# Two interleaved attention and gated-MLP layers on one core: four maxima products together in the lean steps, with three smaller moves in the order

## The chip, the cores and the metric

The kernel runs on one core of a Trainium2 chip. The metric is device time in microseconds (us) for one execution; the kernel before took 2261.78 us (median of 3 runs, 2261.09 to 2262.83).

## What is computed

Two pairs of blocks on x of 2048 x 448, every block with a layer norm before it and a residual after it:

```python
x = x + attention(layernorm(x))   # 16 heads of 28; one key and one value head for all
x = x + (sigmoid(n @ w_gate) * (n @ w_up)) @ w_down   # n = layernorm(x), 1792 wide
# attention: softmax over 2048 keys of (q . k) * 28 ** -0.5, times v, times wo
# and both blocks once more
```

The weights of both layers are the same.

## The kernel before

**Units and steps.** A layer's attention is worked in 16 units of 128 queries (`u`), each in 16 steps of 128 keys (`kt`): 256 steps a layer. A step has four score products, one for a group of four heads (`scores`: tile `s`, line 566; 96 rows deep, because queries and keys are split into high and low halves), four exponentials on ScalarE (`P`, line 570) and four products with the values (`pv`, line 584), of the step before.

**Maxima.** The softmax needs each query's largest score before its unit starts. So beside a unit's steps the next unit's approximate scores are made, 32 rows deep: one group of four heads and 512 keys a step, four products `mx` (line 509; the four heads lie on four row strips of TensorE, `tile_position`), each reduced by VectorE over 512 columns (line 512). `mx_gen` yields after two of the four, so that `next(mx)` is half a group and `group(mx)` a whole one. After 16 groups `maxima` takes the largest (lines 543, 544) and leaves `fin` in `late`; `finish` runs it: a transposition on TensorE (`mt`, line 549), a copy on VectorE (`mr`, line 551) and a DMA on SyncE's queue into row 92 of the next unit's queries `QS` (line 552), which that unit's first score product reads.

**The order.** All orders are written out by hand, and each engine and each DMA queue works in that order. Two strings stand for a pass of two steps: S is a score product, F a slice of other TensorE work (`fill`: query projections, the gated MLP's products), M a group of maxima, m half of one, P the value products, T `finish`, X the end of a step. `FULL` is used where there is much fill work, `LEAN` where there is little: in layer 0 for steps 0 to 49 and in layer 1 for steps 0 to 45, 48 passes of 256 in all. In unit 0 two steps have one more group (`MORE`).

**PSUM.** Score, maxima, fill and transposition tiles share seven PSUM buffers of one tag ("f"); a product waits until the buffer's last reader has finished. An eighth holds `pv`.

**Behind a unit.** Its sums go by stages, one a step (`tick`): `f0` and `fx` move the sums out and back by DMA to spread them, `fy` takes reciprocals (VectorE), `fz` and `fw` move them out and back broadcast (`lb`), `fa` multiplies `pvs` by them on GpSimd (line 675), `fb` splits the product (ScalarE, then VectorE), `fc` starts the product with `wo`. In layer 0's lean steps GpSimd also splits the gate and up weights (lines 154 to 156, 279).

**Queries.** `qproj` projects 512 queries of four heads; the high part is written by ScalarE (line 430) and the low part either by VectorE out of PSUM (line 440), or, where `by_pool` is set, by a second ScalarE write to SBUF (line 433) and GpSimd (line 438). In layer 1 two of its four blocks are projected in the lean steps.

## Time and profile before

| | |
|---|---|
| median of 3 runs | 2261.78 us |
| the profiled execution, its own time | 2257.6 us |
| its span on the core (first to last instruction) | 2255.8 us |
| TensorE busy | 2202.9 us, 98% |
| VectorE busy | 1673.9 us, 74% |
| ScalarE busy | 1397.3 us, 62% |
| GpSimd busy | 1045.8 us, 46% |

Busy time is the time in which an instruction of the engine is under way. TensorE's matmuls overlap, and their ends are modelled, so that a wait can hide in a busy row. In the rows PE is TensorE, PEld its weight loads, DVE is VectorE, ACT ScalarE, POOL GpSimd and SP SyncE; a q behind the name is the engine's DMA queue.

### The profile page before, as it was taken

To read this page: it belongs to the slowest core of one execution; us is meant where nothing else is said; L and a number is where in the kernel's file an instruction comes from. 1 tells how busy PE (TensorE), PEld (TensorE's weight loads), DVE (VectorE), ACT (ScalarE), POOL (GpSimd) and SP (SyncE) were. 2 spreads that over 40 slices of the span, in tenths; PEclk is the share of its full clock that TensorE was granted. 3 is DMA by queue.
4 is the path that set the end of the run, shared out by engine and by line. 5 is a ranking of instruction groups with operands and counts; after the bars stand their busy time and mean duration, and the time that the engine had idled before them with its cause. 6 is when DMAs were issued, how large, how long until landed. Compare 5 with 4: busy or idle time off the path is not lost. (4 is left out here: it accounts for less than half of the span.)

```text
span 2255.8 us, 43048 instructions
## 1 busy us (share of the span) xinstructions
PE 2202.9 (98%) x16336; PEld 1049.5 (47%) x16336; DVE 1673.9 (74%) x2921; ACT 1397.3 (62%) x2567; POOL 1045.8 (46%) x1363
## 2 busy tenths in 40 slices
PE   8999999999999999999999999999999999999999
PEld 6322244544545444454573224545454544445457
DVE  7898887878778887774458887878787877878322
ACT  4677766666666666666425676666666666666641
POOL 4378451555445554546402014545545455454540
PEclk9999999999999999999999999999999999999999
DMA  6734542323313232332341113223232313232233
GB/s 154 212 105 133 184 158 61 93 77 103 112 52 106 67 90 80 98 96 79 102 145 57 31 47 103 85 85 101 60 94 63 102 59 102 80 95 89 78 99 123
DMA packets 224400, 217.53 MB, mean 96 GB/s; under 512 B 154048, under 2 KB 185536, under 8 KB 224192
## 3 DMA queue, kind: packets, MB, share of 16 engines
q1 hardware_dynamic: 217200, 198.89, 30.0%
q0 software_dynamic: 3680, 12.09, 1.4%
q10 hardware_dynamic: 3312, 3.79, 0.5%
q8 instruction: 128, 2.10, 0.4%
q14 instruction: 80, 0.66, 0.1%
HBM read 175.37 MB, written 23.59 MB: 88 GB/s over the span
## 5 line engine op out<-in xcount | busy, mean ns | idle before, releaser
L570 ACT ACTIVATE P<-s 128x512 f32<-128x512 f32 x2048 | 1141.3, 599 | 565.0 <-PE s L566 544.7
L512 DVE TENSOR_REDUCE mp<-mx 128x1 f32<-128x512 f32 x2048 | 1266.7, 681 | 300.6 <-PE mx L509 295.4
L566 PE MATMUL s<-QS,KK 96*128 96x512 f16 x2048 | 740.3, 381 | 21.8 <-DVE mp L512 9.2
L369 PEld LDWEIGHTS <-wgu 128*128 128x128 f16 x4928 | 459.5, 97 | 254.1 <-issue 91.6
L604 POOL TENSOR_TENSOR PH<-P,PH 128x512 f16<-128x512 f32 x384 | 458.7, 1195 | 30.8
L603 POOL CAST PH<-P 128x512 f16<-128x512 f32 x384 | 248.5, 647 | 471.5 <-ACT P L570 471.5
L584 PE MATMUL pv<-P,VV 128*32 128x512 f32 x3328 | 418.5, 599 | 0.0
L369 PE MATMUL gp<-XT,wgu 128*128 128x256 f16 x2464 | 386.1, 272 | 0.8 <-DVE mp L512 0.7
L369 PE MATMUL up<-XT,wgu 128*128 128x256 f16 x2464 | 385.3, 272 | 1.1 <-ACT P L570 0.4
L789 PE MATMUL dn<-WD,h 128*128 128x448 f16 x1344 | 330.4, 353 | 0.0
L509 PE MATMUL mx<-KK,QH 32*128 32x512 f16 x2048 | 257.2, 384 | 5.1 <-ACT P L570 3.1
L566 PEld LDWEIGHTS <-KK 96*128 96x128 f16 x2048 | 188.4, 97 | 136.0 <-issue 62.3
L509 PEld LDWEIGHTS <-QH 32*128 32x128 f16 x2048 | 62.2, 91 | 344.8 <-issue 343.3
L789 PEld LDWEIGHTS <-h 128*128 128x128 f16 x1344 | 124.7, 98 | 138.6 <-issue 23.7
L584 PEld LDWEIGHTS pv<-P,VV 128*32 128x32 f32 x3328 | 86.4, 109 | 167.5 <-issue 146.3
L764 DVE SCALAR_TENSOR_TENSOR h<-th,h 128x512 f16<-128x512 f32 x112 | 99.5, 888 | 48.4 <-ACT h L763 48.4
L763 ACT ACTIVATE h<-th 128x512 f16<-128x512 f32 x112 | 70.3, 628 | 88.0 <-DVE th L760 86.9
L760 DVE SCALAR_TENSOR_TENSOR th<-th,up 128x512 f32<-128x512 f32 x112 | 76.0, 679 | 57.2 <-PE up L369 51.7
L675 POOL TENSOR_TENSOR lb<-pvs,lb 128x512 f32<-128x512 f32 x32 | 40.7, 1270 | 138.3 <-DMA lb<-sums 119.7
L752 ACT ACTIVATE th<-gp,gsc 128x512 f32<-128x512 f32 x112 | 76.8, 686 | 42.3 <-PE gp L369 41.8
L369 PE MATMUL qp<-XT,WQ 128*128 128x512 f16 x352 | 98.4, 386 | 0.7 <-DVE ktl L412 0.7
L329 POOL TENSOR_SCALAR rs<-mv 128x1 f32<-128x1 f32 x48 | 11.0, 229 | 178.6 <-DVE mv L324 178.6
(164 smaller groups left out, 1102.9 us busy)
## 6 DMA issues: line engine op xcount, KB each, us to landing
wgu<-wgu_d SPq DMA_DIRECT2D x224, 512.0 KB
QS<-qd SPq DMA_DIRECT2D x384, 32.0 KB
lb<-sums SPq DMA_DIRECT2D x120, 64.0 KB
wgu_d<-sgu POOLq DMA_DIRECT2D x14, 512.0 KB, 3.8
qd<-qst POOLq DMA_DIRECT2D x16, 256.0 KB, 2.7
xr<-in_A_x_dram SPq DMA_DIRECT2D x16, 224.0 KB
QH<-qd SPq DMA_DIRECT2D x28, 128.0 KB
x2d<-x SPq DMA_DIRECT2D x16, 224.0 KB
```

Of the source, the lines that this page charges most:

```text
L369: nc.tensor.matmul(ps, a, b, start=n == 0, stop=n == 10)
L509: nc.tensor.matmul(ps[h][:, :nk], qh[32 * h:32 * h + 32, g], KK[l][32 * h:32 * h + 32, 1, ks], start=True, stop=True, tile_position=(32 * ...
L512: nc.vector.tensor_reduce(mp[:, g, h, kb:kb + 1], ps[h][:, :nk], axis=AX.X, op=OP.max)
L566: nc.tensor.matmul(s, KK[l][0:96, 0, kt * 128:(kt + 1) * 128], QS[l, u][:, g].rearrange("p h n -> p (h n)"), start=True, stop=True)
L570: nc.scalar.activation(p, s, AF.Exp, scale=ESC)
L584: nc.tensor.matmul(v[32 * g:32 * g + 32], VV[l][:, kt], P[g], start=kt == 0, stop=kt == KT - 1, tile_position=(0, 32 * g))
L603: {"A": nc.scalar.copy, "V": nc.vector.tensor_copy, "P": nc.gpsimd.tensor_copy}[e](h[:, 0], p)
L604: nc.gpsimd.tensor_tensor(h[:, 1], p, h[:, 0], op=OP.subtract)
L752: defer(lambda: nc.scalar.activation(th, gp.rearrange("p j n -> p (j n)"), AF.Tanh, scale=gsc))
L760: nc.vector.scalar_tensor_tensor(t, th, 1.0, up.rearrange("p j n -> p (j n)"), op0=OP.add, op1=OP.mult)
L764: defer(lambda: nc.vector.scalar_tensor_tensor(h[:, 1], t, 2.0 ** -17, h[:, 0], op0=OP.mult, op1=OP.subtract), 1)
L789: nc.tensor.matmul(p, hs[f // 2][:, a, o:o + 128], WD[:, f, c], start=n == 0, stop=n == 3 * FC - 1)
```

## The change

Four edits. `LEAN` has a whole group M at the end of a step, where it had two halves m, one between the score products and one at the end. `finish` leaves `fin` alone until two steps have passed since the group that ended the maxima, except in the last pass of a unit. `fa` comes one step later for units 0 to 2 of each layer (`LU`). And `by_pool` holds for all projections by `qproj`, which moves 12 low parts from VectorE to ScalarE and GpSimd.

```diff
-        by_pool = l == 0 or b == 1
+        by_pool = True
...
-        late.append(fin)
-
-    def finish():
-        while late:
-            late.pop(0)()
+        late.append((at[0], fin))
+
+    at = [0]
+
+    def finish(every=True):
+        while late and (every or at[0] - late[0][0] >= AGE):
+            late.pop(0)[1]()
...
-            return (1, f0), (1, fx), (1, fy), (1, fz), (1, fw), (1, fa), (n, fb), (2, fc)
+            return (1, f0), (1, fx), (1, fy), (1, fz), (1, fw), (1 + (u < LU), fa), (n, fb), (2, fc)
...
+    LU = 3
+    AGE = 2
...
-    LEAN = "FSFSmFSFSPTXmFSFSmFSFSPTXm"
+    LEAN = "FSFSFSFSPTXMFSFSFSFSPTXM"
...
                 elif o == "M":
+                    at[0] = step
                     group(mx)
...
                 elif o == "T":
-                    finish()
+                    at[0] = step
+                    finish(kt >= KT - len(order) // 12)
```

`FULL` passes keep their order of S, M, P and T. The transposition `mt` moves only in lean steps: from behind the value products of step 13 of a unit to behind those of step 14, six times.

On TensorE, in layer 0's first unit, from the last value product ahead of the transposition; before:

```order
L584 MATMUL pv_1548<-P_1998,VV_131 32x512
L549 LDWEIGHTS m16_2022
L549 MATMUL mt_2052<-id16_79,m16_2022 16x128
L509 LDWEIGHTS QH0_139
L509 MATMUL mx_2060<-KK_130,QH0_139 128x512
L509 LDWEIGHTS QH0_139
L509 MATMUL mx_2061<-KK_130,QH0_139 128x512
L566 LDWEIGHTS KK_130
L566 MATMUL s_2067<-QS_1175,KK_130 128x512
L566 LDWEIGHTS KK_130
L566 MATMUL s_2071<-QS_1175,KK_130 128x512
L509 LDWEIGHTS QH0_139
```

and now:

```order
L586 MATMUL pv_1542<-P_2039,VV_131 32x512
L549 LDWEIGHTS m16_2022
L549 MATMUL mt_2082<-id16_79,m16_2022 16x128
L509 LDWEIGHTS QH0_139
L509 MATMUL mx_2087<-KK_130,QH0_139 128x512
L509 LDWEIGHTS QH0_139
L509 MATMUL mx_2088<-KK_130,QH0_139 128x512
L509 LDWEIGHTS QH0_139
L509 MATMUL mx_2093<-KK_130,QH0_139 128x512
L509 LDWEIGHTS QH0_139
L509 MATMUL mx_2094<-KK_130,QH0_139 128x512
L568 LDWEIGHTS KK_130
```

Four maxima products follow each other where two did, then come four score products in a row; between this transposition and the next unit stands one whole step, where there were two.

On GpSimd, in layer 0's second unit, around the first product `lb` with the reciprocals, between the splits of the gate and up weights (`sgu`, `rgu`); before:

```order
L279 DMA wgu_d_104<-sgu_2333 128x2048
L675 TENSOR_TENSOR lb_2382<-pvs_2167,lb_2382 128x512
L154 TENSOR_SCALAR sgu_2463<-rgu_2326,swb_110 128x512
L155 TENSOR_SCALAR rgu_2326<-rgu_2326,swb_110 128x512
L156 TENSOR_TENSOR sgu_2463<-rgu_2326,sgu_2463 128x512
```

and now:

```order
L279 DMA wgu_d_104<-sgu_2327 128x2048
L154 TENSOR_SCALAR sgu_2456<-rgu_2320,swb_110 128x512
L155 TENSOR_SCALAR rgu_2320<-rgu_2320,swb_110 128x512
L156 TENSOR_TENSOR sgu_2456<-rgu_2320,sgu_2456 128x512
L677 TENSOR_TENSOR lb_2376<-pvs_2161,lb_2376 128x512
```

One split of three instructions, which stood behind the product, now stands ahead of it.

On VectorE, at the start of layer 1, around the copy `mr` of the first unit's maxima; before:

```order
L544 TENSOR_SCALAR m16_16683<-m32_16682 128x16
L440 SCALAR_TENSOR_TENSOR qst_16708<-qp_16696,eq_111,qst_16708 128x512
L551 COPY mr_16717<-mt_16715 16x128
L512 TENSOR_REDUCE mp_16720<-mx_16721 128x1
L512 TENSOR_REDUCE mp_16720<-mx_16722 128x1
```

and now:

```order
L544 TENSOR_SCALAR m16_16691<-m32_16690 128x16
L551 COPY mr_16727<-mt_16725 16x128
L512 TENSOR_REDUCE mp_16730<-mx_16731 128x1
L512 TENSOR_REDUCE mp_16730<-mx_16732 128x1
L512 TENSOR_REDUCE mp_16730<-mx_16737 128x1
```

The low part `qst`, which waits for ScalarE's high part, is gone from ahead of the copy.

## Rows read from the trace of the kernel before

**Rows 1.** The page, part 1: busy us (share of the span) and instructions.

```profile
PE 2202.9 (98%) x16336; PEld 1049.5 (47%) x16336; DVE 1673.9 (74%) x2921; ACT 1397.3 (62%) x2567; POOL 1045.8 (46%) x1363
```

**Rows 2.** Windows: both lean stretches whole, and a full one.

```profile
core 0: us, PE busy (x) PEld busy (x) DVE busy (x) ACT busy (x) POOL busy (x), PEclk, DMA share, GB/s
...
105.00:265.30 160.30, 149.35 (x831) 33.92 (x832) 144.97 (x255) 118.15 (x227) 114.09 (x101) 0.99 0.43 132
1211.00:1357.60 146.60, 142.81 (x814) 35.17 (x814) 128.58 (x220) 102.89 (x194) 11.74 (x23) 1.00 0.13 37
...
1400.00:1500.00 100.00, 99.98 (x761) 47.08 (x758) 78.31 (x131) 64.98 (x115) 52.07 (x68) 1.00 0.25 77
```

**Rows 3.** Timeline of PE: a lean step without fill, layer 0. Start us, length us.

```profile
154.43 0.39 PE L509 MATMUL mx<-KK,QH 32*128 32x512 f16 x2
154.75 0.60 PE L566 MATMUL s<-QS,KK 96*128 96x512 f16 x2
155.28 0.39 PE L509 MATMUL mx<-KK,QH 32*128 32x512 f16 x2
155.60 0.61 PE L566 MATMUL s<-QS,KK 96*128 96x512 f16 x2
156.14 1.06 PE L584 MATMUL pv<-P,VV 128*32 128x512 f32 x8
157.14 0.39 PE L509 MATMUL mx<-KK,QH 32*128 32x512 f16 x2
```

**Rows 4.** Timeline of PE: steps 50 and 51, first of the full order, nearly without fill.

```profile
265.30 1.04 PE L566 MATMUL s<-QS,KK 96*128 96x512 f16 x4
266.27 1.06 PE L584 MATMUL pv<-P,VV 128*32 128x512 f32 x8
267.27 0.40 PE L509 MATMUL mx<-KK,QH 32*128 32x512 f16 x4
267.64 1.38 PE L566 MATMUL s<-QS,KK 96*128 96x512 f16 x4
```

**Rows 5.** Timeline of DVE: eight reductions without a pause.

```profile
152.54 4.85 DVE L512 TENSOR_REDUCE mp<-mx 128x1 f32<-128x512 f32 x8
```

**Rows 6.** Windows: steps 8 to 47 of layer 0; columns as in rows 2.

```profile
131.80:259.90 128.10, 119.42 (x674) 27.24 (x673) 116.66 (x197) 91.56 (x174) 106.72 (x95) 1.00 0.44 134
```

**Rows 7.** Waits in the same stretch: us in total, times, longest.

```profile
POOL lb L675 <- DMA lb<-sums: 8.6, 2, 4.5
...
DVE oT L682 <- ACT oT L681: 3.2, 2, 2.0
...
POOL hl L346 <- DVE hl L345: 1.8, 1, 1.8
```

**Rows 8.** Groups by line, layer 1's lean stretch: busy, mean ns, idle before and releasers.

```profile
L512 DVE TENSOR_REDUCE mp<-mx 128x1 f32<-128x512 f32 x191 | 118.6, 682 | 14.7 <-PE mx L509 14.2
...
L509 PE MATMUL mx<-KK,QH 32*128 32x512 f16 x192 | 36.6, 384 | 0.4 <-DVE mp L512 0.2
...
L440 DVE SCALAR_TENSOR_TENSOR qst<-qp,eq,qst 128x512 f16<-128x512 f32 x5 | 3.7, 741 | 0.2 <-ACT qst L430 0.2
```

**Rows 9.** Timelines around three transpositions: layer 0's units 0 and 1, layer 1's unit 0.

```profile
101.74 0.59 ACTq L552 DMA_DIRECT2D QS<-mr  x1
104.96 0.59 PE L566 MATMUL s<-QS,KK 96*128 96x512 f16 x2 [0.23 <-DMA QS<-mr]
151.35 0.22 PE L549 MATMUL mt<-id,m 128*16 128x128 f16 x1
152.41 0.20 DVE L551 COPY mr<-mt 16x128 f16<-16x128 f16 x1
1209.19 0.58 SPq L552 DMA_DIRECT2D QS<-mr  x1
1210.97 0.11 PEld L566 LDWEIGHTS <-KK 96*128 96x128 f16 x2 [0.85 <-DMA QS<-mr]
```

**Rows 10.** Groups by line of the whole run: the low parts' instructions on POOL and ACT.

```profile
L438 POOL TENSOR_TENSOR qst<-qf,qst 128x512 f16<-128x512 f32 x4 | 4.6, 1149 | 5.0 <-ACT qf L433 5.0
L433 ACT ACTIVATE qf<-qp,eq 128x512 f32<-128x512 f32 x4 | 2.7, 680 | 0.0
```

## Prediction

> **What bounds the kernel now.** I read the page's busy times first: TensorE is busy for 98% of the span and VectorE for 74% [rows 1]. In a full stretch, 1400 to 1500 us, TensorE has 99.98 of 100 us [rows 2], so there an edit pays only by taking TensorE work away, and none of the four does that: `FULL` keeps its order, with four maxima products together already. The change lives in the two lean stretches, 160.3 us (layer 0, 25 passes) and 146.6 us (layer 1, 23 passes), 306.9 us in all [rows 2]. There VectorE is busy for 144.97 and 128.58 us, 90% and 88%, and TensorE for 149.35 and 142.81: two engines near their limit.
>
> The timeline of a lean step without fill shows which one sets its length: two pairs of maxima products, two pairs of score products and the value products follow each other without a gap, and the same product returns after 157.14 - 154.43 = 2.71 us [rows 3]. VectorE makes four reductions in such a step; eight in a row take 4.85 us, so four take 2.43 [rows 5]. TensorE is the longer by 0.28 us, and VectorE's idle time ahead of its reductions in layer 1, 14.7 us, nearly all ends with a maxima product [rows 8]. In layer 0 GpSimd is the third: in steps 8 to 47 (128.1 us) it computes for 106.7 us in 95 instructions [rows 6], and of its 21.4 us of idle time only 8.6 + 1.8 us are waits for others [rows 7]; the rest is small gaps between its own instructions. It is in hand for 117.7 of 128.1 us.
>
> **Four maxima products together.** A pair takes 0.32 us to the next product (154.43 to 154.75), and in the steps where four stand together the four take 0.37 (267.27 to 267.64) [rows 3, 4]: the four row strips work at once, and two pairs cost nearly two fours. Step 50 has the new order with almost no fill: four score products, the value products and a four, 265.30 to 267.64, are 2.34 us against 2.71. TensorE saves 0.37 us a group. Layer 1's stretch has 192 maxima products, 48 groups [rows 8]; layer 0's has 50 steps and the two more groups of `MORE`, 52. The saving on TensorE is 17.8 and 19.2 us. That is an upper bound: the step then has 2.34 us of TensorE and 2.43 of VectorE, and VectorE sets it.
>
> The row shows it: a four every 2.34 us feeds reductions that take 2.43. The Trainium skill, TensorEngine Tiling (Array Packing), section PSUM Bottleneck, says the same in general: packing small matrices makes TensorE faster but not the emptying of PSUM, which may become the limit. By TensorE's rows alone the two stretches would give 37 us; by that rule 0.28 us a group, 28 us, less what VectorE has to do beside.
>
> Layer 1: TensorE's 142.8 us less 17.8 leave 125.0; VectorE's 128.6 us less the five low parts (3.7 us, [rows 8]) leave 124.9. Two equal loads that wait on each other through seven PSUM buffers do not both run at 100%. I take 93%, between VectorE's 116.66 of 128.10 us today in layer 0 (91%, [rows 6]) and TensorE's 142.81 of 146.60 (97%, [rows 2]): 125 / 0.93 = 134.4 us, **12.2 us less**. Bounds: 125 us (21.6 less), and 91% with a further waiting of 5 us from the row of score products that spread to 1.38 us behind a four, 0.4 more than 0.97 [rows 4] (4 less).
>
> Layer 0: in steps 8 to 47 VectorE has 116.7 us and GpSimd 117.7, so this part cannot go much below 118 while the weights are split in it; I take 121, between that and 128.1 (7 less). The 32 us around it, ten steps, give 0.28 us a step at best; I take 2. Together **9 us less**, bounds 3 and 15 (VectorE's 144.97 of 160.3 is the floor, [rows 2]).
>
> **The product with the reciprocals a step later.** In layer 0 GpSimd waits 8.6 us in two places for the broadcast sums, VectorE 3.2 us behind it [rows 7]. The order now puts one more split ahead of the product; it is work that GpSimd has to do anyway, so its wait nearly vanishes while the product ends no earlier. That is how GpSimd's 117.7 us can hold as a floor when the steps get shorter, and it is counted in the 121. TensorE's product with `wo` comes a step later; other work stands in its place. Without this edit the wait would grow by about what the steps lose, 0.28 us for each of some six steps.
>
> **Low parts by GpSimd.** Twelve low parts leave VectorE (741 ns each, [rows 8]) for ScalarE (680 ns) and GpSimd (1149 ns) [rows 10]. In layer 1's lean stretch GpSimd has 11.7 us of work and ScalarE 102.9 of 146.6 [rows 2]: hidden, and VectorE's 3.7 us are counted above. The four for layer 1's first block fall in full steps where VectorE does not bind: nothing. At layer 1's start ScalarE does one more 0.68 us write ahead of its first exponentials, while the copy of the maxima loses the low part ahead of it, which frees the first score product from its 0.85 us wait [rows 9]. I let these cancel; either alone is the bound.
>
> **The transposition later.** Six times the maxima are transposed one step later, so that TensorE does not wait for a VectorE that now lags. What is left of the way: from the transposition to the next unit's first score product there were two steps and are now one, with a four: about 0.2 + 0.37 + 2.34 = 2.9 us. Needed are the copy, which ended 152.61 - 151.35 = 1.26 us after the transposition began, and the DMA: 1.8 us from issue to its reader in layer 1 (1209.19 to 1210.97), at most 3.2 in layer 0 (101.74 to 104.96) [rows 9]. That makes 3.0 to 4.5 us, a wait of 0.1 to 1.6 us, six times: 0.6 to 9.6 us. Queued behind it are all of TensorE's products; VectorE has up to two fours in hand meanwhile. I take 0.35 us each, near the low end, because the reductions in hand cover part: **2 us more**.
>
> **Sum.** 12.2 + 9 - 2 = 19.2 us. The profiled execution took 2257.6 us; it would take 2238.4. It lies 4.2 us below the median of the runs, 2261.78, so the median forecast is 2242.6 us.
>
> **Rivals.**
> - *VectorE and GpSimd keep the pace.* Layer 0 hardly moves (2 us), because both are in hand for 117 of 128 us; layer 1 runs at 91% (125 / 0.91 = 137.4, 9.2 less); the transpositions cost 4. For it: the row of 2.43 us and the floor of GpSimd. Against: VectorE still has 15.3 and 18.0 us of idle time in the stretches. Gain 7 us: 2255. The Trainium skill's rule on PSUM's emptying, above, points this way.
> - *The whole of TensorE's saving comes through.* 21.6 us in layer 1, 15 in layer 0, no wait: 2225. Against: VectorE would have to be busy without a pause.
> - *The fours are not fours.* A four needs four of seven PSUM buffers, the score products want four more, and where the third is still being reduced the four falls into two pairs. For it: four score products after a four took 1.38 us instead of 0.97 in step 51 [rows 4]; 0.4 us of waiting a step eats the 0.37. Gain 2 us, from the low parts: 2260, no change that can be told.
> - *Slower.* The maxima's row arrives late at six unit starts. Should the copy stand behind a whole four of reductions (2.43 us more) and the DMA take 3.2, the way is 1.26 + 2.43 + 3.2 = 6.9 us against 2.9, a wait of 4 us, 24 us in all, against a gain that it cuts to 16, as VectorE runs dry behind each wait: 2270. It decides from 16 / 6 = 2.7 us a start on. Against it: the copy stands ahead of the new four in the order.
>
> **Chances.** Forecast 0.58 (its own range 2236 to 2250), VectorE and GpSimd 0.22, whole saving 0.06, no fours 0.08, slower 0.06. A measurement of this kernel tells about 0.2% (4.5 us) from no change. The first three are faster: 0.86; the fourth is the same: 0.08; slower 0.06. The range that leaves out the last two and the whole saving is 2232 to 2256.
>
> **What will show it.** Right: lean passes of 2 x 2.45 to 2 x 3.0 us (about 6.0 us a pass in layer 0 for 6.4, 5.8 in layer 1 for 6.4); the maxima products' busy time in layer 1's stretch down from 36.6 us to about 19; VectorE's reductions there the same 118.6 us, with the idle time ahead of them down from 14.7 to about 6; TensorE with visible idle time in lean stretches that ends with VectorE; full stretches unchanged to a microsecond. Wrong: score products that wait for `QS` at units 1 to 3 by over 1 us each, fours spread over 0.6 us, or GpSimd's splits ending later than layer 0's step 50.

## The result, and the profile after

The changed kernel takes 2262.81 us (median of 12 runs, 2259.86 to 2265.44), the kernel before 2260.53 (12 runs beside it): a ratio of 1.0019, 95% interval 1.001 to 1.0028. (The two medians alone would give 1.0010; the ratios here and below are those on record with the intervals.) It is slower by a little, where 2242.6 was forecast. The profiled span grew by 6.4 us, from 2255.8 to 2262.2.

The page's busy times, as in [rows 1]:

```profile
PE 2189.0 (97%) x16336; PEld 1047.4 (46%) x16336; DVE 1664.1 (74%) x2909; ACT 1400.5 (62%) x2579; POOL 1063.0 (47%) x1375
```

TensorE has 13.9 us less to do, and the span did not fall. Windows of the two lean stretches, of the steps 50 to 82 of layer 0 and 46 to 82 of layer 1 behind them, and of layer 0's steps 8 to 47; columns as in [rows 2]:

```profile
103.90:261.70 157.80, 139.27 (x834) 33.59 (x833) 143.16 (x252) 116.26 (x226) 115.11 (x101) 0.96 0.42 130
1212.60:1360.70 148.10, 136.60 (x815) 34.10 (x814) 123.84 (x211) 103.78 (x199) 18.15 (x29) 0.99 0.14 37
261.70:398.40 136.70, 132.72 (x946) 62.52 (x943) 104.11 (x185) 91.78 (x167) 44.71 (x53) 0.99 0.38 122
1360.70:1502.00 141.30, 139.55 (x1052) 66.21 (x1049) 109.08 (x184) 93.19 (x167) 75.77 (x94) 1.00 0.29 86
130.40:256.30 125.90, 111.36 (x672) 26.76 (x671) 114.97 (x195) 90.33 (x174) 106.60 (x95) 0.96 0.42 130
```

The same steps of the kernel before:

```profile
265.30:397.40 132.10, 130.29 (x944) 62.25 (x943) 104.92 (x183) 90.77 (x167) 43.90 (x53) 1.00 0.38 121
1357.60:1496.20 138.60, 138.18 (x1051) 66.04 (x1050) 109.09 (x183) 92.42 (x165) 73.54 (x92) 1.00 0.29 87
```

So layer 0's lean stretch fell from 160.3 to 157.8 us, layer 1's grew from 146.6 to 148.1, and the steps behind them grew by 4.6 and 2.7. In layer 1's lean stretch TensorE has 92% of the time and VectorE 84%: neither is full any more. The groups by line of that stretch show what each lost:

```profile
L512 DVE TENSOR_REDUCE mp<-mx 128x1 f32<-128x512 f32 x189 | 117.2, 683 | 23.3 <-PE mx L509 22.9
...
L568 PE MATMUL s<-QS,KK 96*128 96x512 f16 x184 | 62.5, 382 | 9.2 <-DVE mp L512 8.5
...
L509 PE MATMUL mx<-KK,QH 32*128 32x512 f16 x192 | 21.3, 388 | 1.8 <-DVE mp L512 1.6
```

The maxima products fell from 36.6 to 21.3 us [rows 8]: the fours are fours. But VectorE now idles 23.3 us ahead of its reductions, for 14.7, and TensorE's score products wait 8.5 us in turn for reductions, for 1.6 before. The timeline of TensorE shows where in a step:

```profile
1275.52 0.39 PE L509 MATMUL mx<-KK,QH 32*128 32x512 f16 x4
1275.84 0.39 PE L568 MATMUL s<-QS,KK 96*128 96x512 f16 x1
1276.07 0.38 PE L369 MATMUL qp<-XT,WQ 128*128 128x512 f16 x1
1276.29 0.77 PE L568 MATMUL s<-QS,KK 96*128 96x512 f16 x2
1277.28 0.38 PE L568 MATMUL s<-QS,KK 96*128 96x512 f16 x1 [0.22 <-DVE mp L512]
1277.58 1.07 PE L586 MATMUL pv<-P,VV 128*32 128x512 f32 x8
1278.58 0.39 PE L509 MATMUL mx<-KK,QH 32*128 32x512 f16 x4
```

and that of VectorE:

```profile
1272.87 2.48 DVE L512 TENSOR_REDUCE mp<-mx 128x1 f32<-128x512 f32 x4 [0.64 <-PE mx L509]
1275.94 2.48 DVE L512 TENSOR_REDUCE mp<-mx 128x1 f32<-128x512 f32 x4 [0.58 <-PE mx L509]
```

A step is 1278.58 - 1275.52 = 3.06 us, while its reductions take 2.48. The fourth score product waits for a reduction of the four just ahead of it (the second of them ends by these rows at 1277.2); behind it stand the value products, 1.0 us, and only then the next four. VectorE has run dry by then. Each engine waits for the other in turn. The median of the stretch's 46 steps is 3.07 us, for 3.15 before; but the two steps with one more group take 5.1 us each, for 3.8.

In layer 0 another wait came, at the end of step 41. The timelines of GpSimd, ScalarE and TensorE:

```profile
231.65 0.62 POOL L279 DMA_DIRECT2D wgu_d<-sgu  x1 [0.30 <-POOL sgu L156]
232.30 1.27 POOL L677 TENSOR_TENSOR lb<-pvs,lb 128x512 f32<-128x512 f32 x1
```

```profile
233.61 0.62 ACT L683 CAST oT<-lb 128x512 f16<-128x512 f32 x1 [6.06 <-POOL lb L677]
```

```profile
229.77 0.39 PE L509 MATMUL mx<-KK,QH 32*128 32x512 f16 x1
234.77 1.10 PE L509 MATMUL mx<-KK,QH 32*128 32x512 f16 x3 [4.62 <-ACT P L572]
235.80 1.89 PE L568 MATMUL s<-QS,KK 96*128 96x512 f16 x4
```

The product `lb` stands behind a split that GpSimd, busy with the splits before it, got to late; ScalarE stands still for 6.06 us ahead of the copy of it, its exponentials queue behind that, the buffers of the score tiles stay full, and TensorE waits 4.62 us in the middle of a four. Afterwards four score products take 1.89 us, where [rows 4] have 1.04. A window that begins 1.2 us before the wait ends shows the granted clock at 0.50:

```profile
233.60:240.40 6.80, 5.63 (x21) 1.09 (x21) 3.36 (x6) 4.75 (x9) 6.53 (x5) 0.50 0.76 289
```

### The profile page after: what moved, and what is told of

The parts are those of the page before. It is cut to its first block, busy times and chain, and to the rows that moved or that the text cites. A ratio compares the mean times of both kernels' runs of the same rounds, so it can differ in the third digit from the quotient of the medians.

```text
span 2262.2 us, 43093 instructions
## 1 busy us (share of the span) xinstructions
PE 2189.0 (97%) x16336; PEld 1047.4 (46%) x16336; DVE 1664.1 (74%) x2909; ACT 1400.5 (62%) x2579; POOL 1063.0 (47%) x1375
## 4 chain that ended last, share of the span: by engine, by line
PE 78%; DVE 10%; DMA 3%; ACT 3%; issue 2%; POOL 2%; SPq 2%; DVEq 0%; ACTq 0%; POOLq 0%
PE s L568 17%; PE pv L586 15%; PE dn L791 11%; PE up L369 10%; PE gp L369 10%; DVE mp L512 8%; PE mx L509 6%; PE pv L582 3%; PE wo L699 3%; PE qp L369 2%; ACT P L572 2%; SPq L469 1%; DMA XT<-hl 1%; DMA lb<-sums 1%; DVE th L762 0%
## 5 line engine op out<-in xcount | busy, mean ns | idle before, releaser
L568 PEld LDWEIGHTS <-KK 96*128 96x128 f16 x2048 | 192.5, 97 | 148.1 <-issue 62.1
L509 PE MATMUL mx<-KK,QH 32*128 32x512 f16 x2048 | 227.9, 386 | 13.1 <-ACT P L572 5.8
L509 PEld LDWEIGHTS <-QH 32*128 32x128 f16 x2048 | 55.0, 91 | 317.9 <-issue 316.8
L791 PEld LDWEIGHTS <-h 128*128 128x128 f16 x1344 | 124.7, 98 | 138.7 <-issue 23.7
```

Source lines behind the costliest of these rows:

```text
L509: nc.tensor.matmul(ps[h][:, :nk], qh[32 * h:32 * h + 32, g], KK[l][32 * h:32 * h + 32, 1, ks], start=True, stop=True, tile_position=(32 * ...
L568: nc.tensor.matmul(s, KK[l][0:96, 0, kt * 128:(kt + 1) * 128], QS[l, u][:, g].rearrange("p h n -> p (h n)"), start=True, stop=True)
L791: nc.tensor.matmul(p, hs[f // 2][:, a, o:o + 128], WD[:, f, c], start=n == 0, stop=n == 3 * FC - 1)
```

## The experiments

Each time below is a median beside runs of the kernel before on the same chip. The stretches are worked out from the starts of the first score products of the steps named (layer 0: steps 0 to 50 and 50 to 82; layer 1: 0 to 46 and 46 to 82), of one profiled execution each. Layer 0's lean stretch differs by up to 5.1 us between kernels of the same order there (e7, e8, e10 and e16; by 4.4 between e3, e9 and e13), so that no single difference of that size is read from it; the others differ by 1 to 2.

| kernel | median us | ratio to before, 95% | L0 lean | 50 to 82 | L1 lean | 46 to 82 |
|---|---|---|---|---|---|---|
| before | 2260.53 | | 160.3 | 132.1 | 146.6 | 138.6 |
| after | 2262.81 | 1.0019 (1.001 to 1.0028) | 157.8 | 136.7 | 148.1 | 141.2 |
| e1 fours alone | 2266.8 | 1.0035 (1.0022 to 1.0049) | 163.8 | 132.2 | 149.8 | 139.2 |
| e2 after with pairs | 2260.58 | 1.0013 (1.0 to 1.0027) | 157.5 | 137.7 | 147.3 | 140.8 |
| e3 after, product early | 2256.9 | 0.9993 (0.9984 to 1.0003) | 160.1 | 132.1 | 149.3 | 138.8 |
| e4 after, four first | 2270.59 | 1.0053 (1.0037 to 1.0068) | 165.0 | 134.6 | 148.0 | 140.7 |
| e5 low parts alone | 2259.2 | 1.0004 (0.999 to 1.0018) | 164.8 | 132.1 | 147.2 | 138.7 |
| e6 product later alone | 2262.71 | 1.002 (1.0009 to 1.0032) | 164.7 | 136.3 | 146.5 | 140.8 |
| e7 transposition alone | 2263.58 | 1.0018 (1.0006 to 1.003) | 160.8 | 132.1 | 146.8 | 139.0 |
| e8 low parts and transposition | 2259.9 | 1.0011 (0.9998 to 1.0025) | 161.5 | 132.1 | 147.3 | 138.6 |
| e9 fours, fill held | 2265.07 | 1.003 (1.0021 to 1.0039) | 158.2 | 132.2 | 143.5 | 149.7 |
| e10 pairs, fill held | 2268.07 | 1.0044 (1.003 to 1.0058) | 164.1 | 132.1 | 149.9 | 149.2 |
| e11 fours, six buffers | 2372.1 (one run) | | 163.9 | 141.5 | 165.5 | 147.8 |
| e12 pairs, six buffers | 2360.93 (one run) | | 167.1 | 138.9 | 160.4 | 147.3 |
| e13 fours, fill closed and held | 2250.7 | 0.9955 (0.9938 to 0.9971) | 162.6 | 132.3 | 130.3 | 147.3 |
| e14 values after two scores | 2267.06 | 1.0036 (1.0023 to 1.0049) | 165.3 | 132.3 | 150.3 | 139.2 |
| e15 values after three scores | 2265.16 | 1.0031 (1.0017 to 1.0045) | 160.7 | 132.2 | 149.1 | 138.7 |
| e16 pairs, fill closed and held | 2259.27 | 0.9997 (0.9981 to 1.0013) | 165.9 | 132.1 | 137.0 | 147.0 |
| e17 e13 with GpSimd relieved | 2252.88 (one run) | | 158.2 | 131.7 | 132.0 | 147.3 |
| e18 change whole, fill closed and held | 2254.68 | 0.9979 (0.9966 to 0.9993) | 156.5 | 135.1 | 130.8 | 149.6 |

Most of that spread goes with the granted clock. Its mean over layer 0's lean stretch is 0.99 in the kernel before, e2, e7 and e8, 0.97 in e9 and e10, 0.96 in the changed kernel, e3, e5, e16 and e18, 0.95 in e13, 0.94 in e1 and 0.93 in e6. The length times this mean is an estimate of what the stretch would take at full clock (it counts half of all time at 0.50 as lost, so it can go too low): 158 to 160 us for pairs with the product early (before, e5, e7, e8, e10, e16), 153 to 155 for fours with it early (e1, e3, e9, e13), 150 to 152 for fours with it late (after, e18).

**e1 to e4: parts of the change.** e1 puts the new order into the kernel before, e2 the old order into the changed kernel, e3 the product back to its old step, e4 the four ahead of the value products.

```diff
 e1, on before:  -    LEAN = "FSFSmFSFSPTXmFSFSmFSFSPTXm"
                 +    LEAN = "FSFSFSFSPTXMFSFSFSFSPTXM"
 e2, on after:   the same, reversed
 e3, on after:   -    LU = 3
                 +    LU = 0
 e4, on after:   -    LEAN = "FSFSFSFSPTXMFSFSFSFSPTXM"
                 +    LEAN = "FSFSFSFSMPTXFSFSFSFSMPTX"
```

> The kernel before with the new lean order alone. Theory A (buffers): right behind a four the score products have to wait for that four's own reductions, since eight tiles a step share seven buffers; a lean step stays at 2.9 to 3.1 us in layer 1 and the fours give nothing: 2258 to 2263 us. Theory B (GpSimd behind): the fours are good, and the loss after the change came from ScalarE's 6 us wait for a product with reciprocals that now stands behind a weight split; without that edit the gain appears: 2248 to 2254 us. Theory C (late maxima): the transposition at its old place makes TensorE wait 1 to 2 us at six places, 2264 to 2270 us.

> The kernel after with pairs again in the lean order; the three other edits stay. Theory A: the other edits alone are worth what VectorE is relieved of, 2255 to 2260 us, and the score products' waits for reductions (20.7 us over the run after the change) fall back to about 9. Theory B: the product behind the split costs its 6 us wait here too, 2262 to 2267 us.

> The kernel after with the product with the reciprocals at its old step (LU = 0). Theory A: layer 1 stays as after the change, 148 us in its lean stretch, layer 0 changes by 2 us or less: 2261 to 2264 us. Theory B: the 6.1 us wait of ScalarE and the 4.6 us wait of TensorE in layer 0's third unit go, and with them two records of the half clock there: layer 0's lean stretch 151 us or less for 157.8, 2254 to 2258 us.

> The kernel after with the four ahead of the value products in a lean step (S S S S M P T X for S S S S P T X M): the value products need no buffer, and give VectorE 1.0 us more before the next score product wants one. Theory A: score products no longer wait for reductions of the four ahead; a lean step in layer 1 falls from 3.07 to 2.6 to 2.8 us, the stretch from 148 to 134 to 140 us, in all 2245 to 2254 us. Theory B or a limit by VectorE alone: the place of the four in the step does not matter, 2260 to 2265 us.

The fours alone lose 0.35%; in neither layer does a stretch with fours come out clearly under one with pairs, as measured. By the whole time e1 fits theory C and e3 theory B, but their stretches don't: layer 0's in e3 stayed at 160.1 us where theory B had 151 or less, and layer 1's at 149.3, as theory A had it. e2 came out between its theories; its score products wait 1.4 us for reductions in layer 1's stretch. Taking the product back (e3) gives 4.6 us of layer 0's steps 50 to 82 and 2.4 us of layer 1's 46 to 82 back. Part of e1's loss is the transposition, early again: TensorE waits for it 3.6 us in layer 0's lean stretch and 1.6 us in layer 1's (its waits for `m`, line 544), and not at all in e3.

e4 is the slowest. With the four ahead of the value products its score products wait 0.7 us for reductions in layer 1's stretch, not 8.5, but the fours come apart, as TensorE's timeline and its groups show:

```profile
1279.92 0.60 PE L568 MATMUL s<-QS,KK 96*128 96x512 f16 x2
1280.45 0.74 PE L509 MATMUL mx<-KK,QH 32*128 32x512 f16 x4
1281.13 1.06 PE L586 MATMUL pv<-P,VV 128*32 128x512 f32 x8
```

```profile
L509 PE MATMUL mx<-KK,QH 32*128 32x512 f16 x192 | 39.0, 378 | 3.5 <-ACT qf L433 1.1 <-DVE mp L512 0.4
```

Four products take 0.74 us there and 39.0 us in all, as much as pairs. So the place of the four decides whether it is one; why the third and fourth follow late is not shown by any releaser.

**e5 to e8: the other edits alone.**

```diff
 e5, on before:  -        by_pool = l == 0 or b == 1
                 +        by_pool = True
 e6, on before:  -(1, fw), (1, fa), (n, fb)
                 +(1, fw), (1 + (u < 3), fa), (n, fb)
 e7:             the changed kernel with e5's line, LU and LEAN as before
 e8:             the changed kernel with LU and LEAN as before
```

> The kernel before with one edit: all low parts by GpSimd. Theory S (each edit has its own price, the same in any company): VectorE's load in layer 1's lean stretch falls by the five low parts, 3.7 us, but with pairs TensorE holds that stretch (142.8 of 146.6 us), so it falls by 1 us at most; layer 1's first score product loses its wait of 0.85 us; the whole is 1 to 2 us below the kernel before, ratio 0.999 to 1.000. Theory I (the edits are free alone and cost only in each other's company): no difference above 0.5 us in any stretch. Rival G: GpSimd's low parts come 0.4 us later each and hold layer 1's start back: first 16 steps of layer 1 over 52 us against 50.6, ratio above 1.001.

> The kernel before with one edit: the product with the reciprocals one step later for the first three tiles. Theory S: this edit alone lengthens layer 0's steps 50 to 82 from 132 us to 136 to 138 (that is where the two kernels with it had 136.7 and 137.7 and the three without it 132.1 to 134.6), while steps 24 to 40 shorten by about 5 us to 46 to 48 because GpSimd's weight splits stand ahead of the product; lean stretch of layer 0 about 158; the whole 0 to 4 us above the kernel before, ratio 1.000 to 1.002. Theory I: 132 us in steps 50 to 82, time equal to the kernel before within 1 us. If steps 40 to 50 grow from 33.6 to 36 us or more here, the late product behind the splits delays the first units' tail whether or not the maxima products come in fours.

> The kernel before with one edit: the maxima's transposition a step later, with pairs. Theory S: the two half steps that remain leave the maxima's row just in time; the score products of the next unit wait for it 0 to 0.8 us six times; time 0 to 2 us above the kernel before, ratio 1.000 to 1.001. Theory I: nothing, within 0.5 us in the lean stretches (160.3 and 146.6 us). Rival L (late row): waits of over 1 us at units 1 to 3, 6 us or more in all, ratio above 1.002.

> The changed kernel with pairs again and the product at its old step, so that only the low parts and the transposition differ from the kernel before. Theory S: the sum of those two alone, 0 to 2 us below the kernel before, ratio 0.999 to 1.000, and 1 to 3 us below the run with the product a step later beside them (2260.6 us). Theory I: equal to the kernel before within 1 us. If it is 3 us or more below the kernel before it is the best version so far.

The low parts make no difference. The later product costs 4.3 us alone. Layer 0's steps 50 to 82 grow as expected, and so do layer 1's 46 to 82, which the expectation did not name. Layer 0's steps 24 to 40 shorten as expected, from 51.3 to 47.3 us, but its lean stretch took 164.7 where about 158 was expected: its first eight steps took 33.8 for 26.8, at a mean granted clock of 0.70 for 0.94. The reason for the loss is not more work; windows of e6 with the same steps as above:

```profile
269.40:405.70 136.30, 132.57 (x944) 62.74 (x943) 102.98 (x183) 91.75 (x168) 44.65 (x53) 0.99 0.37 118
1367.00:1507.80 140.80, 139.42 (x1048) 66.09 (x1047) 109.02 (x183) 92.09 (x165) 73.29 (x92) 1.00 0.29 86
```

TensorE has the same 944 products in layer 0's 32 steps, and they take 132.57 us for 130.29, with 1.9 us more of idle time. Some 1.7 of these 2.3 us of busy time are the clock, an estimate: its mean is 0.51 from 275.0 to 278.4 us, behind a wait of 0.23, and all of that time is busy. Not all of the loss is: e18's window has a clock of 1.00 and takes 135.1 us, 2.8 over e13's; and e6's in layer 1, 2.2 us longer than before, has 1.00 too. The stage with `wo` now falls into another step of the full order, and its neighbours meet small waits; that this is the reason was not tried by itself. e7 loses 0.18%, though its profiled execution shows the four stretches unchanged within 0.5 us. The 4.0 us by which its span is longer lie mostly where its order is that of the kernel before: 1.3 ahead of layer 0's first step, and 2.1 between step 82 and layer 1's start, where the clock stood at 0.50 from 1145.8 to 1149.2 us. Whether the edit causes this stays open. With the low parts beside it (e8) the interval reaches 1.

**e9 to e12: without fill, and with one buffer less.** In e9 (fours) and e10 (pairs), both with the product early, layer 1's lean steps make no query projections; these come behind step 46. e11 is e3 and e12 is e8 with one buffer less, their fill as before. From here on theory B is the one on buffers, theory A of e1 to e4.

```diff
-            order = FULL if rate > LEANR else LEAN
+            order = FULL if (step >= 46 if l else rate > LEANR) else LEAN
...
-                    fill.slice(rate * 2 / order.count("F"))
+                    fill.slice(0 if l and order is LEAN else rate * 2 / order.count("F"))
 e11, e12:
-    NBK = {"f": 7, "s": 2, "m": 3}
+    NBK = {"f": 6, "s": 2, "m": 3}
```

> Fours, with the product at its old step; the projections that fill layer 1's lean stretch are held back until its step 46 (TensorE's some 20 us of them come in the full stretch behind it). Theory B (buffers): without fill a step asks for eight tiles of the seven buffers, and no projection sits on one of them for eight steps; the last score product then waits for the first reduction of the four ahead, not for its second or third; a step takes 2.45 to 2.65 us, the stretch 118 to 125 us instead of 149, the whole 2245 to 2254 us. Theory H (hand-over): VectorE idles 0.4 to 0.6 us ahead of each four, because the four is handed over in one piece, with or without fill; a step stays at 2.9 us or more, the stretch at 135 us or more, and as the 20 us come back later the whole is at 2262 us or more.

> The same with pairs, for comparison. Both theories: a pair step without fill takes 2.71 us, as in the kernel before, so the stretch takes 126 to 131 us instead of 147, and with the 20 us of projections behind it the whole is 2259 to 2264 us. Theory B says that the run with fours and held fill is at least 6 us below this one, theory H that it is above it.

> Fours, with the product at its old step, and six buffers instead of seven for all of score, maxima and fill tiles. Theory B: one buffer less makes two score products of a step wait for one more reduction each (0.62 us), the step grows by 0.4 to 0.6 us and layer 1's lean stretch from 149 to 167 us or more. Theory H: the hand-over stays, the stretch grows by less than 8 us.

> Pairs with six buffers instead of seven. Theory B: two tiles at a time leave more slack, the stretch grows from 147 us by less than it does with fours, to 150 to 160 us. Theory H: pairs and fours lose alike.

By time e9 spoke for the hand-over, and its step is that of the changed kernel. But its timeline shows two score products that wait, each for one reduction:

```profile
1262.66 0.39 PE L509 MATMUL mx<-KK,QH 32*128 32x512 f16 x4
1262.99 0.60 PE L568 MATMUL s<-QS,KK 96*128 96x512 f16 x2
1263.83 0.38 PE L568 MATMUL s<-QS,KK 96*128 96x512 f16 x1 [0.23 <-DVE mp L512]
1264.42 0.38 PE L568 MATMUL s<-QS,KK 96*128 96x512 f16 x1 [0.22 <-DVE mp L512]
1264.73 1.07 PE L586 MATMUL pv<-P,VV 128*32 128x512 f32 x8
1265.73 0.40 PE L509 MATMUL mx<-KK,QH 32*128 32x512 f16 x4
```

That gives the step exactly: 1.76 us from the four to the last score product, 0.31 to the value products, 1.00 to the next four, 3.07. And it shows why holding the fill did not help. The fill stops in the middle of a projection, whose tile keeps a buffer all the while; in the order of e9 every tile of the stretch goes to the six others. Eight tiles a step on six buffers: the third score product takes the buffer of the first maxima product just ahead of it. In the changed kernel a projection's tile is held so too, 24 to 41 us each from its first product to its last reader, one behind the other for 96% of the stretch.

e10, pairs on six buffers, missed as well: 149.9 us where 126 to 131 was expected. But most of this is the clock and not the buffer: its mean over the stretch is 0.92, and for 17 us on end, behind waits of 0.55, 0.22 and 0.15 us, it stood at 0.50. The stretch and that window:

```profile
1211.98:1361.89 149.91, 143.52 (x763) 31.20 (x763) 125.89 (x214) 100.24 (x191) 10.42 (x21) 0.92 0.11 30
1231.50:1248.60 17.10, 17.10 (x58) 2.16 (x56) 9.51 (x15) 7.38 (x14) 0.00 (x0) 0.50 0.00 0
```

At full clock a step of its pairs takes 2.72 us, as expected, although the tile is open:

```profile
1217.13 0.39 PE L509 MATMUL mx<-KK,QH 32*128 32x512 f16 x2
...
1219.85 0.39 PE L509 MATMUL mx<-KK,QH 32*128 32x512 f16 x2
```

With all of it at full clock the stretch would take some 138 us, an estimate (149.9 times 0.92), less than the 143.5 of the fours. The medians of e9 and e10 are too close to part them (the intervals overlap). e11 and e12 show the price of a buffer beside fill: some 16 us in this stretch with fours (149.3 to 165.5), 13 with pairs (147.3 to 160.4), and over 100 us in the whole. Theory B's numbers for them were near, 167 or more and 150 to 160; theory H's growth of less than 8 us was not.

**e13, e16, e18: the buffer given back.** e13 is e9 with the projection in hand finished before its fill is held. e16 is e13 with pairs, e18 is e13 with `LU = 3`, that is the whole change.

```diff
             yield from qproj(l, XT, b, g)
+            yield 0
...
         fill.slice(QCH)
+        while l:
+            c = next(fill.gens[0][0])
+            fill.debt -= c
+            fill.gens[0][1] -= c
+            if not c:
+                fill.debt = 0.0
+                break
```

> The run with fours and held fill again, with one difference: at layer 1's start the projection in hand is finished before its fill is held, so that no half projection sits on a buffer during the stretch (in the run before it one did; its steps took 3.07 us without any fill, two score products each waiting for one reduction of the four just ahead). Theory B (buffers): with the seventh buffer free only the last score product can meet the first reduction, steps take 2.45 to 2.65 us, layer 1's lean stretch 46 x 2.55 + 3 = 118 to 126 us instead of 143.5, the whole 2245 to 2252 us. Theory H (hand-over in one piece): 2.9 to 3.07 us a step, 140 us or more, whole at 2262 us or more.

> The control of the run at 2250.7 us: the same closed and held fill, but pairs. If the gain there came from the fours on a free buffer (theory B), a pair step stays at TensorE's 2.71 us, layer 1's lean stretch takes 127 to 131 us plus the later fill, and as the fours' alternate steps had waits of 0.8 us the two may lie close: pairs 132 us against 130.3, whole 2250 to 2258 us. If it came from the held fill alone, pairs are as fast or faster: 126 us or less, 2248 us or less.

> The changed kernel whole, all four edits, with layer 1's projection closed and its fill held: does the change pay where its fours have their buffers? Theory B with the measured price of the later product (4 to 4.5 us in layer 0's steps 50 to 82, some 2 us in layer 1's, less what steps 24 to 40 give back): layer 1's lean stretch 130 us as in the run at 2250.7 us, the whole 2252 to 2256 us, ratio 0.997 to 0.999. Rival: the later product costs more where steps are short; 2258 us or more.

e13 is 0.45% faster than the kernel before, as theory B had it. Its timeline of TensorE, and then the windows of e9, e13 and e16 for layer 1's lean stretch:

```profile
1290.41 0.39 PE L510 MATMUL mx<-KK,QH 32*128 32x512 f16 x4
1290.73 1.22 PE L569 MATMUL s<-QS,KK 96*128 96x512 f16 x4
1291.88 1.06 PE L587 MATMUL pv<-P,VV 128*32 128x512 f32 x8
1292.88 0.40 PE L510 MATMUL mx<-KK,QH 32*128 32x512 f16 x4
1293.21 0.82 PE L569 MATMUL s<-QS,KK 96*128 96x512 f16 x3
1294.81 0.38 PE L569 MATMUL s<-QS,KK 96*128 96x512 f16 x1 [0.79 <-DVE mp L513]
```

```profile
1209.60:1353.10 143.50, 123.89 (x764) 29.13 (x764) 123.87 (x211) 98.80 (x191) 10.45 (x21) 1.00 0.12 31
```

```profile
1212.70:1343.00 130.30, 122.22 (x763) 29.61 (x761) 122.28 (x209) 98.31 (x191) 11.21 (x22) 0.99 0.12 34
```

```profile
1218.10:1355.10 137.00, 133.46 (x763) 29.77 (x761) 123.72 (x213) 99.64 (x191) 11.11 (x22) 0.99 0.12 32
```

e9 and e13 have the same work in the stretch, within a product and within two microseconds on every engine; the one differs by a buffer, and takes 13.2 us less. A step without a wait takes 2.47 us, what four reductions take, and the median of the 46 is 2.50, as expected; the wait shown, in a step of 3.24, comes where VectorE has 0.9 us of other work ahead of the four's reductions. Ten steps take 3.0 to 5.2 us, and so the stretch came out at 130.3 where 118 to 126 was expected. VectorE and TensorE are both busy for 94%. The pairs of e16 have the same buffers and hold the stretch at TensorE's 133.46 us, 97% of 137.0; both this and the whole, even with the kernel before, lie above what was expected, and their median step is 2.71 us, no shorter than with the tile open in e10. So at full clock the free buffer takes 0.6 us off a step of fours and nothing off a step of pairs, and the gain of e13 over e16 is that of the fours, on a buffer that is free, and not that of the held fill; some of it lies in layer 0, by the estimate below the table. By the medians the open tile costs 14.4 us with fours (e9, e13) and 8.8 with pairs (e10, e16); of the latter only the profiled execution can be read, and it puts most of the difference on the clock. e18 shows the same of the whole change: 0.21% faster than before, as expected, and 4 us behind e13 (on another chip), of the size of the later product's price.

**e14, e15: the value products moved up.** Both are e3 with one string changed, to cover the score products' waits.

```diff
 e14: +    LEAN = "FSFSPFSFSTXMFSFSPFSFSTXM"
 e15: +    LEAN = "FSFSFSPFSTXMFSFSFSPFSTXM"
```

> Fours, with the product at its old step, and the value products between the second and the third score product of a step instead of behind the fourth. Theory B: the two score products that wait for reductions of the four just ahead come 1.0 us later, when these reductions are done; but the last two of the next four take the buffers of the score products just ahead of them, whose exponentials they must wait for. If only the first holds, steps take 2.6 to 2.75 us, layer 1's stretch 125 to 133 us, layer 0's 150 us, the whole 2232 to 2245 us; if the wait for the exponentials takes its place, steps stay at 2.95 to 3.1 us and the whole at 2255 to 2265 us. I hold the second for likelier, as the fours placed directly behind the score products lost. Theory H: no change from 149 us in layer 1.

> The same with the value products between the third and the fourth score product. Theory B: the fourth is covered, the third still waits 0.2 us; only the last buffer of the next four belongs to the score product directly ahead of it. Steps of 2.75 to 2.95 us, layer 1's stretch 130 to 140 us, the whole 2240 to 2252 us. Theory H: no change from 149 us.

The wait moves. In e14 score products wait 1.8 us for reductions, but the maxima products take 28.1 us for 21.3 and the four meets the wait itself, as its timeline shows:

```profile
1293.33 0.60 PE L568 MATMUL s<-QS,KK 96*128 96x512 f16 x2
1293.86 0.39 PE L509 MATMUL mx<-KK,QH 32*128 32x512 f16 x3
1295.05 0.37 PE L509 MATMUL mx<-KK,QH 32*128 32x512 f16 x1 [0.80 <-DVE mp L512]
1295.65 0.38 PE L568 MATMUL s<-QS,KK 96*128 96x512 f16 x1 [0.23 <-DVE mp L512]
```

The expected cause, a wait of the maxima products for exponentials, is 1.2 us in that stretch; the fourth product of the four waits for a reduction here. In e15 the stretch stayed at 149.1 us, where theory B had 130 to 140 and theory H no change; score products wait 4.1 us for reductions. With eight tiles a step and the projection's long-lived one on seven buffers, each of these orders only chose which product waits.

**e17: layer 0.** It leaves out GpSimd's scaling of the gate and up weights, so that their low parts are taken from unscaled values.

```diff
     def split_pp(hi, lo, src, s):
         nc.gpsimd.tensor_scalar(hi, src, s, None, op0=OP.mult)
-        nc.gpsimd.tensor_scalar(src, src, s, None, op0=OP.mult)
         nc.gpsimd.tensor_tensor(lo, src, hi, op=OP.subtract)
```

> The run at 2250.7 us without GpSimd's scaling of the gate and up weights ahead of their low parts (left out: 21 instructions of 1.59 us, 33 us, in layer 0's lean stretch). Theory G (GpSimd, in hand for 117 of 128 us, is the floor of layer 0's lean stretch, as the prediction had it): steps 8 to 50 fall from 135.9 us to 120 to 127 us, VectorE's 119 us being the next. Theory V (VectorE's reductions, the splits between them and TensorE's waits set it): they stay within 4 us, at 132 us or more.

Steps 8 to 50 take 131.0 us instead of 135.9. Windows of e13 and of e17 there:

```profile
129.60:265.50 135.90, 120.73 (x705) 28.34 (x705) 122.99 (x206) 94.75 (x185) 107.50 (x95) 0.95 0.43 135
```

```profile
133.50:264.50 131.00, 118.63 (x705) 28.20 (x705) 119.80 (x203) 94.67 (x185) 73.67 (x74) 0.96 0.46 141
```

34 us less on GpSimd give 4.9 us in one execution, no more than these steps differ between kernels with one order there (134.4 to 139.4 us in e7, e8, e10 and e16), and the steps take more than the 127 us of theory G: GpSimd is not what holds them up. VectorE stays at 91% of the time; what keeps it there was not settled.

## Why the prediction was wrong

**Layer 1, 12.2 us less: the step that failed first.** It took TensorE's and VectorE's loads after the saving, found them equal at 125 us, and let them run at 93%. TensorE's saving is there: the maxima products take 21.3 us, near the 19 forecast. But the stretch takes 148.1 us where 134.4 was forecast, and VectorE, said to set it, is busy for 84%. The step asked how much work each engine has and not which product needs which buffer when. The kernel's `qp` tile keeps a buffer for eight steps and more, six are left for eight tiles, and a score product waits for a reduction of the four just ahead of it, with the value products between it and the next four. That chain, 3.07 us, is longer than a step of pairs without fill, 2.71 [rows 3] and 2.72 in e10 beside the same open tile, and e9 shows that it needs no fill work, only the buffer. With the buffer free (e13) the occupancy of both engines is 94%, nearly the figure taken.

**The rival that came nearest** was that the fours are not fours, at 2260: its rows, four score products that spread behind a four [rows 4], were the right ones, its 0.4 us a step the right size. Only the fours did stay fours, and the loss stood behind them. The Trainium skill, TensorEngine Tiling (Array Packing), section Gotcha 1: PSUM Pressure, says that row tiles write to different PSUM banks and so press on PSUM; here e9 against e13 puts 13.2 us on one buffer. Of the same page of the Trainium skill the prediction weighed the section PSUM Bottleneck, on emptying PSUM: its rate is not what bound here, since VectorE was idle for 23.3 us ahead of its reductions.

**Layer 0, 9 us less:** 2.5 came in this execution, less than like kernels differ by; runs with fours and runs with pairs lie side by side there (156.5 to 167.1). Its floor, GpSimd in hand for 117 us, is hardly one (e17). The stretch's granted clock is 0.96, where the kernel before has 0.99 [rows 2], and the sum put the clock at nothing. By the estimate of length times clock the two stretches are 151.5 and 158.7 us: some 7 of the 9 us came, and nearly 5 of them went to the clock. No run has fours at 0.99 there, so this is not shown, nor that the fours lower the clock: e5 and e16, with pairs, have 0.96 too.

**The product a step later, counted at nothing:** wrong by 4 to 6 us in three comparisons of the ratios (e6 with the kernel before, the change with e3, e18 with e13); between e2 and e8, the fourth, it is 0.5 us. "Its wait nearly vanishes while the product ends no earlier" overlooked that it may end later. ScalarE's wait of 3.1 us at step 24 fell to 0.4, but at step 41 the product stood behind a late split, and a wait of 6.06 us on ScalarE, where the kernel before has 2.7 at step 40, became one of 4.62 on TensorE. And the units of the full stretch behind were taken as unchanged to a microsecond, while e6 shows 4.2 and 2.2 us there; from step 82 on layer 0 is in fact unchanged.

**The transposition later, 2 us more:** mis-sized. No unit's first score product waits for the maxima's row longer than before, and beside the fours the edit removes the 5.2 us for which TensorE waits in e1. Alone it costs 0.18%; in the profiled execution that lies where the order is unchanged, and its cause stays open.

**Low parts, nothing:** right (e5). **Slower through a late maxima row:** no such wait came.

The sum by measured terms, in the profiled spans: -2.5 + 1.5 in the lean stretches, +4.6 + 2.7 behind them, together 6.3 of the 6.4 us. These are two single executions: the medians lie 2.3 us apart, and the -2.5 is within what like kernels differ by.

## What to carry to other kernels

When products are grouped to run at once, count the tiles of a step against the buffers, the long-lived ones too, and follow the chain from the group through the last product that reuses one of its buffers to the next group; that chain, not either engine's load, sets the step. Finish or keep out a tile that sits on a buffer before making the groups larger: here the order alone lost, held fill and a free buffer with pairs came out even with the kernel before, and with fours they gained 0.45%. An edit that moves a short step later isn't free because its engine is waiting: look at who stands still behind it, and at the tuned stretch into which its successors fall. Before two stretches are compared, read the granted clock of both: in e10 a stretch at 0.92 looked like the price of a buffer.

## What the runs showed of the hardware

- The granted clock fell from full speed to 0.50, that is from 2.4 to 1.2 GHz, at or behind waits of TensorE. It fell near the end of the one of 4.62 us and stood there until 240.4 us, and products took up to twice their time: four score products 1.89 us instead of 1.04. A second place is in layer 0's unit 0, where ahead of it, from 121.84 us on, four products had waited 0.22 to 0.23 us each for reductions:

```profile
124.40:127.80 3.40, 3.40 (x16) 0.55 (x15) 3.40 (x6) 1.83 (x4) 1.41 (x1) 0.50 0.02 5
```

The kernel before shows a mean of 0.99 in that lean stretch, the changed one 0.96; with full speed in the places of both rows the products would have saved some 4.5 us there, an estimate, half of 3.4 and 5.63 us busy. e13 has 0.95 and is faster all the same.

- Four row-strip products took 0.39 us directly behind value products (1275.52) and 0.74 behind score products (e4, 1280.45), with no releaser named. Whether that is a buffer or the row strips that the score products use too was not tried.
